# A fourth place for w1's low parts, later transposes of gathered rows, later loads of expert 0's weights, and constant products in TensorE's planned gaps

## The chip, the cores and the metric

The kernel runs on one core of one Trainium2 chip. The metric is the device time of one execution in microseconds (us); lower is better. The engines are called as the profile calls them: PE is TensorE (PEld its weight loads), DVE is VectorE, ACT is ScalarE, POOL is GpSimd and SP is SyncE, whose queue here issues nearly all DMAs.

## The reference

Three stages follow each other: an attention with random features, a dense two-layer block on all 2304 tokens, and a layer of 8 experts with 288 tokens each. Inputs are float32, two dense weight matrices arrive as float64.

```python
# attention: q, k, v are 4 x 8 x 576 x 64, omega 128 x 64
q_p, k_p = phi(q * scale), phi(k * scale)        # exp(x.omega - |x|^2/2 - max) / sqrt(128)
num = q_p @ (k_p^T v);  den = q_p . sum(k_p) + 1e-6
x = (num / den)                                  # 2304 x 512
# dense block: w_in 512 x 2048, w_out 2048 x 512
h = x @ w_in;  x = (h - tanh(h)) @ w_out
# experts: w_gate 512 x 8, w1 8 x 512 x 1024, w2 8 x 1024 x 512
logits = x @ w_gate                              # tokens go to experts in the order of all logits,
                                                 # each expert takes 2304 / 8 = 288 tokens
out[mask_e] = maximum(x[mask_e] @ w1[e], 0) @ w2[e]
```

## The kernel before

Every matrix product is made from three products of high and low parts (high x high, high x low, low x high). So every weight is split: the high part is a rounded copy (ACT), the low part a subtraction (DVE or POOL).

The program is not written in the order in which it runs. Each piece of work is an `op` with an engine (or several to choose from), a planned duration, a priority (`plan.at` plus `lag`), the buffers that it reads and writes and other ops that it follows. `Plan.run` is a list scheduler: it takes the op that can start first by its own model of the engines and issues it. This fixes the order of instructions on each engine; at run time an engine takes them in that order and waits where something is late. Buffers are rings of places (`Ring`), and an op that needs a new buffer waits in the plan until a place is free. `late` adds time to the planned end of an op, and so moves what depends on it back in the plan.

In order of time:

- From 0 to about 125 us: the attention (`unit_ops`), its units mixed with the conversion of the float64 weights (`weight_ops`: DVE reads the bits, ACT makes the high part, DVE or POOL the low part). The key units add into accumulators of the ring `kvr`, of which the first 260 of 512 columns are used.
- To about 533 us: the dense block in 6 blocks of 384 tokens (`mlp_ops`), 16 chunks (f) each: `chunk_ops` makes the hidden values, `m2_ops` (L651) multiplies them with w_out. Blocks 4 and 5 run their first product together, from about 450 us. The products of block 4 with w_out come later, so its low hidden parts go to DRAM, one store for each chunk (`g4l<-gL`, L826). In the same stretch `low_ops` makes the low parts of the first two of four row groups of w1 of all experts, 16 pieces: load of 512 KB (`dw`, L581), two copies on ACT into `dh`, two subtractions on DVE or POOL in place, store to `w1l` (L588). The ring `dw` has 3 places, `dh` 2.
- At about 534 us: a branch (`tc.If`, L1530) that goes to a general version of the dense block when inputs are out of a range; with this input it is passed by. SP's instruction at its end waits for the semaphores of all eight of its DMA queues, that is until everything that SP issued has landed; the other engines go on when SP has.
- To about 622 us: `but_last_ops` and `last_ops`, block 4's and block 5's products with w_out (low parts `oL` loaded from DRAM through 3 places), mixed with the routing of the first expert (`route_ops`: a search whose steps go PE L1096, DVE, PE L1121, DVE) and the second's. When the first expert's tokens are known, POOL gathers their rows (`r_xg`, `xg_rest`, L1351), and PE transposes them (L1369).
- To the end: 8 experts (`expert_ops`), while the next ones are searched for, gathered (L1351, transposes L1364) and their weights loaded (`load_ops`, L1309 to L1330). Expert 0's loads are tied to the loads of `oL` (`oloads`): load number i of its weights follows oL load 2i + 2, the low part follows 2i + 3.

Of the kernel before, what the change touches and what calls it, by code (L numbers as in the profile page):

```python
# [65 lines left out]
class Plan:  # L66
# [6 lines left out]
    def __init__(self):  # L73
        self.ops, self.n, self.at = [], 0, 0.0
        self.free = dict.fromkeys(("PE", "ACT", "DVE", "POOL", "SP", "-"), 0.0)
        self.dma = 0.0
        self.rings = []

    def ring(self, shape, dtype, name, slots):
# [49 lines left out]
    def run(self):  # L129
# [5 lines left out]
        while count:  # L135
# [19 lines left out]
            for b in o.new:  # L155
                if b.slot is not None:
                    continue
                s = self._place(b, (), o.new)
                b.slot, s[4] = s, b
                b.t = s[0].tile(b.ring.shape, b.ring.dtype, tag=s[1], name=s[1], bufs=1)  # L160
            o.fn(e)
            ready.remove(o)
# [24 lines left out]
def tile_kernel(ctx, tc, q, k, v, omega, w_in, w_out, w_gate, w_gate_t, w1, w2, out, dbg=None):  # L187
# [5 lines left out]
    P = 128  # L193
# [110 lines left out]
    def low(e, out, in_, high):  # L304
        (nc.gpsimd if e == POOL else nc.vector).tensor_tensor(out, in_, high.bitcast(F32), op=OP.subtract)  # L305
# [16 lines left out]
    pair = lambda z: z.t.rearrange("p n two -> p (n two)")  # L322
    wbuf, stored_low, first_lo = {}, {}, {}
    bwn, bxn, bhm = Buf(None), Buf(None), Buf(None)

    def weight_ops(kind, f, rings, masked=None):
# [14 lines left out]
        if masked:  # L341
# [3 lines left out]
            plan.op(DVE, 0.6, lambda e: V.copy_predicated(w.t, mk.t.bitcast(I32), masked[1]), r=[w, mk], w=[w])  # L345
        plan.op(ACT, 0.6, lambda e: copy(e, dst.t, w.t), r=[w], w=[dst], lag=6.6)
        plan.op({POOL: 1.4, DVE: 0.7}, 0, lambda e: low(e, lw.t, w.t, dst.t), r=[w, dst], w=[lw], lag=7.3)
# [225 lines left out]
    def low_ops(start, step):  # L573

        n = w1.shape[2]
        d_rings[:] = plan.ring([P, n], F32, "dw", []), plan.ring([P, n // 2], F32R, "dh", [])
        for k in range(E * NPRE):
            e_, r = k // NPRE, slice(k % NPRE * P, (k % NPRE + 1) * P)
            raw = Buf(d_rings[0])
            plan.at = start + step * k  # L580
            plan.op(SP, 0.47, lambda e, raw=raw, e_=e_, r=r: nc.sync.dma_start(raw.t, w1[e_, r, :]), w=[raw], nbytes=P * n * 4,  # L581
                    early=False)
            for i, h in enumerate((slice(0, n // 2), slice(n // 2, n))):
                hi = Buf(d_rings[1])
                plan.op(ACT, 0.6, lambda e, raw=raw, hi=hi, h=h: copy(e, hi.t, raw.t[:, h]), r=[raw], w=[hi], lag=4.0 + 0.6 * i)
                plan.op({POOL: 1.45, DVE: 0.65}, 0, lambda e, raw=raw, hi=hi, h=h: low(
                    e, raw.t.bitcast(F32R)[:, h], raw.t[:, h], hi.t), r=[raw, hi], w=[raw], lag=4.7 + 0.6 * i)
            plan.op(SP, 0.47, lambda e, raw=raw, e_=e_, r=r: nc.sync.dma_start(w1l[e_, r, :], raw.t), r=[raw],  # L588
                    nbytes=P * n * 4, lag=6.8)
# [75 lines left out]

    def gate_ops(j, xms):
        mT, lp, lT, lgb = Buf(mTr), Buf(bank), Buf(sr), Buf(None)
# [20 lines left out]

        plan.op(PE, 0.9, gate, r=[mT, bwg], w=[lp], lag=4.0)
        plan.op({ACT: 0.48, DVE: 0.55}, 0, lambda e: copy(e, lT.t, lp.t[:, :BLK]), r=[lp], w=[lT], lag=5.0)  # L690
# [67 lines left out]
    def mlp_ops(start, step, general=False):  # L758
# [4 lines left out]
        for j in range(NBLK - 1):  # L763
# [34 lines left out]
            plan.at = start[j] + step[j] * NF + LAG2  # L798
            gate_ops(j, xms)

# [498 lines left out]
    def load_ops(p, ei):  # L1299
# [4 lines left out]
        for i in range(2 * NC):  # L1304
# [10 lines left out]
            plan.at = PHASE * p + AT_EW * i + AT_LOAD  # L1315
            turn = [] if p else [oloads[min(2 * i + 2, NF - 1)]]
            plan.op(SP, 0.47, load, w=[raw], after=[o] + turn, nbytes=P * FX * 4)
            plan.at = PHASE * p + AT_EW * i + (AT_SPLIT if p else 0.0)
            plan.op(ACT, 0.98, lambda e, H=H, raw=raw: copy(e, H.t, raw.t), r=[raw], w=[H])
            if i < NPRE:  # L1320
# [3 lines left out]
                plan.at = PHASE * p + AT_EW * i + (AT_SPLIT - 6.0 if p else AT_LOAD)  # L1324
                turn = [] if p else [oloads[2 * i + 3]]
                plan.op(SP, 0.47, load_low, w=[L], after=[o] + turn, nbytes=P * FX * 4)
# [16 lines left out]
    def expert_ops(p):  # L1343
# [4 lines left out]
        for g in range(NG):  # L1348
            t = tmp([GS, DM], F32, "xg", NG - 1) if g < NG - 1 else first["xg"]
            ix = idxs[p][g][1] if p else first["top"][g]  # L1350
            plan.op(POOL, 1.03, lambda e, g=g, t=t, ix=ix: nc.gpsimd.indirect_dma_start(  # L1351
                out=t.t[:GN[g]], out_offset=None, in_=ms if p else ms[:(NTT - TPB) * P + 1, :],
                in_offset=bass.IndirectOffsetOnAxis(ap=ix.t[:GN[g]].bitcast(U32), axis=0)),
                r=[ix], w=[t], after=stored if p else stored4, late=5.0)
            xg.append(t)
# [99 lines left out]

    plan.op(PE, 6.0, warm, w=[idle])
    plan.at = -20.0
    omega_ops()
# [39 lines left out]
    def switch(e):  # L1498
        s_px.close()
        pacc = Lasting(pool(s_acc, "pacc", "right", space=PSUM))  # L1500
        accr.add(pacc, [f"acc{t}" for t in range(TPB)], t=max(o.end for o in early_ops))

    def switch2(e):
        s_att.close()
# [8 lines left out]

    low_ops(starts[-2], (NF * steps[-1] + 4.0) / (E * NPRE))
    plan.at = T_MLP
    plan.op("-", 0.0, switch, after=early_ops)
    mlp_ops(starts, steps)
    att_ops += x_reads
    plan.op("-", 0.0, switch2, after=att_ops)
# [149 lines left out]
```

## Time and profile before

| | |
|---|---|
| time, median of 3 runs | 891.68 us (891.31 to 892.25) |
| the profiled execution's own time | 886.79 us |
| its span, first to last instruction | 884.9 us |
| PE busy | 846.3 us (96%) |
| DVE busy | 654.1 us (74%) |
| ACT busy | 470.2 us (53%) |
| POOL busy | 252.9 us (29%) |

Times below are counted from the span's start. Busy PE is not PE at its peak: the clock that was granted to it has two levels, 1.2 and 2.4 GHz, which the profile shows as 0.5 and 1.0. An engine's wait counts for the end only where nothing later takes it up.

### The profile page before, as it was taken

How to read it: one execution, taken by the hardware profiler on the slowest of the kernel's cores; microseconds unless marked ns; L12 is line 12 of the kernel's file. 1: busy time of each engine (PE TensorE's matmuls, PEld its weight loads, DVE VectorE, ACT ScalarE, POOL GpSimd, SP SyncE). 2: the span in 40 equal slices, each digit the busy share in tenths (PEclk: the TensorE clock that was granted, in tenths of full speed). 3: DMA queues.
4: the chain of work that ended last, by engine and by line, in shares of the span. 5: the costliest groups of instructions: out<-in, count | busy, mean ns of one | idle time of the engine just before them, and what ended most of it. 6: DMA issues, size and time to landing. Idle time of an engine off the chain costs nothing. (4 is left out here: it accounts for less than half of the span.)

```text
span 884.9 us, 17420 instructions
## 1 busy us (share of the span) xinstructions
PE 846.3 (96%) x6116; PEld 756.0 (85%) x6116; DVE 654.1 (74%) x1925; ACT 470.2 (53%) x1021; POOL 252.9 (29%) x276
## 2 busy tenths in 40 slices
PE   8979899999999999999999997989999999999995
PEld 6878788888988888889988985766999988999995
DVE  5898999886588889887887884444887877886520
ACT  4876564744456554755477870012565465455621
POOL 1122344222343345334521251010132322321211
PEclk8999999999999999999999997999999999999998
DMA  8988778887456666633478865567879778877600
GB/s 255 341 259 276 265 240 277 301 264 225 114 184 206 200 191 198 231 100 119 131 265 275 283 229 181 185 230 225 242 233 273 241 207 271 286 207 280 220 27 27
DMA packets 103790, 193.95 MB, mean 219 GB/s; under 512 B 28305, under 2 KB 42257, under 8 KB 103698
## 3 DMA queue, kind: packets, MB, share of 16 engines
q1 hardware_dynamic: 98034, 173.92, 59.7%
q0 software_dynamic: 5664, 18.88, 8.6%
q8 instruction: 49, 0.80, 0.4%
q14 instruction: 43, 0.35, 0.1%
HBM read 149.64 MB, written 33.69 MB: 207 GB/s over the span
## 5 line engine op out<-in xcount | busy, mean ns | idle before, releaser
L604 PE MATMUL bk<-xH,wi 128*128 128x384 f32 x332 | 118.3, 356 | 1.4 <-DVE xt L503 1.1
L605 PE MATMUL bk<-xL,wi 128*128 128x384 f32 x332 | 111.9, 337 | 0.5 <-DVE xL L305 0.5
L606 PE MATMUL bk<-xH,iL 128*128 128x384 f32 x332 | 112.0, 337 | 0.0
L651 PE MATMUL acc<-wo,gL 128*128 128x512 f32 x282 | 111.8, 397 | 0.0
L721 DVE SCALAR_TENSOR_TENSOR lw<-wf,raw 128x512 f32<-128x512 f32 x128 | 107.3, 838 | 5.4 <-POOL wf L718 4.0
L651 PE MATMUL acc<-wo,gH 128*128 128x512 f32 x240 | 99.9, 418 | 0.0
L305 POOL TENSOR_TENSOR gL<-s,gH 128x384 fp32r<-128x384 f32 x49 | 58.1, 1186 | 138.4 <-ACT gH L300 138.4
L441 ACT ACTIVATE phi<-bk,nm 128x128 f32<-128x128 f32 x272 | 77.2, 380 | 36.5 <-DVE nm L444 36.2
L651 PE MATMUL acc<-oL,gH 128*128 128x512 f32 x240 | 95.6, 398 | 0.3 <-DVE oL L305 0.3
L718 POOL TENSOR_TENSOR wf<-oL,wo 128x512 f32<-128x512 f32 x48 | 66.5, 1387 | 66.2 <-DMA oL<-low_wo 55.9
L300 ACT ACTIVATE gH<-s 128x384 fp32r<-128x384 f32 x80 | 42.0, 525 | 62.0 <-DVE s L631 37.1
L604 PEld LDWEIGHTS bk<-xH,wi 128*128 128x128 f32 x332 | 62.9, 189 | 9.0 <-issue 2.0
L629 DVE SCALAR_TENSOR_TENSOR s<-s,bk 128x384 f32<-128x384 f32 x83 | 45.4, 548 | 32.1 <-ACT s L628 31.9
L605 PEld LDWEIGHTS bk<-xL,wi 128*128 128x128 f32 x332 | 62.8, 189 | 3.2 <-DVE xL L305 0.7
L651 PEld LDWEIGHTS acc<-wo,gL 128*128 128x128 f32 x282 | 53.3, 189 | 12.2
L608 ACT ACTIVATE u<-bk 128x384 f32<-128x384 f32 x80 | 39.2, 490 | 44.0 <-PE bk L606 42.7
L606 PEld LDWEIGHTS bk<-xH,iL 128*128 128x128 f32 x332 | 62.6, 189 | 0.0
L631 DVE SCALAR_TENSOR_TENSOR s<-s,u 128x384 f32<-128x384 f32 x80 | 54.6, 682 | 1.1
L444 DVE TENSOR_REDUCE nm<-bk 128x4 f32<-128x512 f32 (+1 forms) x75 | 46.3, 632 | 12.2 <-PE bk L430 11.1
L651 PEld LDWEIGHTS acc<-wo,gH 128*128 128x128 f32 x240 | 45.6, 190 | 7.0 <-issue 0.3
L651 PEld LDWEIGHTS acc<-oL,gH 128*128 128x128 f32 x240 | 45.6, 190 | 6.3 <-DVE oL L305 0.6
L628 ACT ACTIVATE s<-u,qbias 128x384 f32<-128x384 f32 x80 | 49.3, 617 | 2.0
(409 smaller groups left out, 2336.9 us busy)
## 6 DMA issues: line engine op xcount, KB each, us to landing
r_wraw<-in_moe_w_dram SPq DMA_DIRECT2D x50, 512.0 KB, 5.7
iL<-low_wi SPq DMA_DIRECT2D x80, 256.0 KB, 3.3
oL<-low_wo SPq DMA_DIRECT2D x78, 256.0 KB, 2.8
raw<-in_moe_w_in_dram SPq DMA_DIRECT2D x32, 512.0 KB, 5.3
raw<-in_moe_w_out_dram SPq DMA_DIRECT2D x32, 512.0 KB, 4.1
dw<-in_moe_w_dram SPq DMA_DIRECT2D x16, 512.0 KB, 5.3
w1l<-dw SPq DMA_DIRECT2D x16, 512.0 KB, 3.7
s_wraw<-in_moe_w_dram SPq DMA_DIRECT2D x14, 512.0 KB, 6.8
```

The lines of the kernel that those rows point to most:

```text
L305: (nc.gpsimd if e == POOL else nc.vector).tensor_tensor(out, in_, high.bitcast(F32), op=OP.subtract)
L441: nc.scalar.activation(ph.t[:, i0 + i, :], pj.t[:, i * M:(i + 1) * M], AF.Exp, bias=nmx.t[:, i0 + i:i0 + i + 1])
L444: plan.op(DVE, 0.1 + 0.125 * n, lambda e, pj=pj, i0=i0, n=n: V.tensor_reduce(nmx.t[:, i0:i0 + n], pj.t[:, :n * M].rearrange("p (i m) -> p ...
L604: nc.tensor.matmul(ph(), piece(iH, c), xH.t[:, c, :], start=(c == 0), stop=False)
L605: nc.tensor.matmul(ph(), piece(iH, c), xL.t[:, c, :], start=False, stop=False)
L606: nc.tensor.matmul(ph(), piece(iL, c), xH.t[:, c, :], start=False, stop=(c == NC - 1))
L628: plan.op(ACT, 0.52, lambda e: nc.scalar.activation(s.t, ut(), AF.Square, bias=qbias), r=[u], w=[s], lag=2.8)
L629: plan.op(DVE, 0.52, lambda e: V.scalar_tensor_tensor(s.t, s.t, QD, ph(), op0=OP.add, op1=OP.mult), r=[p, s], w=[s], lag=3.4)
L631: plan.op(DVE, 0.65, lambda e: V.scalar_tensor_tensor(s.t, s.t, QC, ut(), op0=OP.mult, op1=OP.mult), r=[u, s], w=[s], lag=4.0)
L651: nc.tensor.matmul(acc[t].t, (gL if k == 2 else gH).t[:, c], (oL if k == 1 else oH).t, start=(f == 0 and k == 0), stop=(f == end and k == ...
L718: plan.op(POOL, 1.45, lambda e: nc.gpsimd.tensor_tensor(w.t, lo.t.bitcast(F32), wo[:, f, :].bitcast(F32), op=OP.add), r=[lo, wbuf["wo", f] ...
L721: x_reads.append(plan.op(DVE, 0.9, lambda e, i=i: nc.vector.scalar_tensor_tensor(scratch.t.bitcast(F32), w.t, 1.0, half(rows[i // 2], i % ...
```

## The change

1. `low_ops` is planned to be done 12 us earlier (its step is computed with -8.0 in place of +4.0), and once block 3's logits are made, the tile `mT` that they were made from becomes a fourth place of the ring `dw`. The two ACT copies of a piece are now planned ahead of its two subtractions, which no longer count as dependent on each other.
2. The gather's planned end is 8.0 us after its issue for expert 0 (5.0 before) and 6.5 us for the others, so the transposes stand later in PE's order.
3. Expert 0's weight loads follow oL loads 2i + 6 and 2i + 7 in place of 2i + 2 and 2i + 3.
4. Until the last weight is converted, where the plan leaves PE idle for over 0.9 us, up to 18 products of constants (128 columns each, bf16) are issued there. They add into columns 384 to 511 of a key accumulator, which nobody reads. In this program there are 42 of them in five places (8, 6, 10, 7 and 11).

```diff
@@ Plan.run
+            if e == "PE" and self.fill and t - self.free[e] > 0.9:
+                self.fill(min(0.4 * (t - self.free[e]), 1.0))
             o.fn(e)
@@ low_ops
-            for i, h in enumerate((slice(0, n // 2), slice(n // 2, n))):
-                hi = Buf(d_rings[1])
+            halves = [(h, Buf(d_rings[1])) for h in (slice(0, n // 2), slice(n // 2, n))]
+            for i, (h, hi) in enumerate(halves):
                 plan.op(ACT, 0.6, lambda e, raw=raw, hi=hi, h=h: copy(e, hi.t, raw.t[:, h]), r=[raw], w=[hi], lag=4.0 + 0.6 * i)
+            for i, (h, hi) in enumerate(halves):
                 plan.op({POOL: 1.45, DVE: 0.65}, 0, lambda e, raw=raw, hi=hi, h=h: low(
-                    e, raw.t.bitcast(F32R)[:, h], raw.t[:, h], hi.t), r=[raw, hi], w=[raw], lag=4.7 + 0.6 * i)
+                    e, raw.t.bitcast(F32R)[:, h], raw.t[:, h], hi.t), r=[hi], rp=[raw], wp=[raw], lag=4.7 + 0.6 * i)
@@ before gate_ops
+    class Whole:
+        def __init__(self, z):
+            self.z = z
+        def tile(self, shape, dtype, tag, **kw):
+            return self.z.rearrange("p c n -> p (c n)")[:, :shape[1]]
@@ gate_ops
-        plan.op(PE, 0.9, gate, r=[mT, bwg], w=[lp], lag=4.0)
+        o = plan.op(PE, 0.9, gate, r=[mT, bwg], w=[lp], lag=4.0)
+        if j == NBLK - 3 and not general:
+            plan.op("-", 0.0, lambda e: d_rings[0].add(Whole(mT.t), ["x"], t=o.end), after=[o])
@@ load_ops
-            turn = [] if p else [oloads[min(2 * i + 2, NF - 1)]]
+            turn = [] if p else [oloads[min(2 * i + 6, NF - 1)]]
...
-                turn = [] if p else [oloads[2 * i + 3]]
+                turn = [] if p else [oloads[2 * i + 7]]
@@ expert_ops, the gather
-                r=[ix], w=[t], after=stored if p else stored4, late=5.0)
+                r=[ix], w=[t], after=stored if p else stored4, late=6.5 if p else 8.0)
@@ tile_kernel
+    def spare(us):
+        accs = [s[4] for s in kvr.slots if s[4] is not None]
+        if accs:
+            fresh = not any(o.done for o in accs[0].writers)
+            for i in range(int(us / 0.055)):
+                nc.tensor.matmul(accs[0].t[:, P * 3:], onev.to_broadcast([P, P]), onev.to_broadcast([P, P]),
+                                 start=fresh and not i, stop=False, skip_group_check=True)
+    plan.fill = spare
...
+    def switch1(e):
+        plan.fill = None
...
-    low_ops(starts[-2], (NF * steps[-1] + 4.0) / (E * NPRE))
+    low_ops(starts[-2], (NF * steps[-1] - 8.0) / (E * NPRE))
...
+    plan.op("-", 0.0, switch1, after=[high_op["wo", NF - 1]])
```

The first place is SP's queue just ahead of the branch, before the change; `w1l<-dw` stores a low part of w1, `dw<-` loads the next piece, `g4l` are block 4's hidden low parts.

```order
L588 DMA w1l<-dw_6360 128x1024
L826 DMA g4l_92<-gL_6488 128x384
L826 DMA g4l_93<-gL_6506 128x384
L588 DMA w1l<-dw_6400 128x1024
L581 DMA dw_6533<-in_moe_w_dram 128x1024
L588 DMA w1l<-dw_6457 128x1024
L826 DMA g4l_94<-gL_6541 128x384
L588 DMA w1l<-dw_6533 128x1024
L1529 TENSOR_LOAD over
```

The same place of the changed kernel (its lines 584, 592 and 841 are 581, 588 and 826 of before).

```order
L584 DMA dw_6438<-in_moe_w_dram 128x1024
L841 DMA g4l_90<-gL_6448 128x384
L841 DMA g4l_91<-gL_6462 128x384
L592 DMA w1l<-mT_5732 128x1024
L841 DMA g4l_92<-gL_6508 128x384
L592 DMA w1l<-dw_6378 128x1024
L841 DMA g4l_93<-gL_6542 128x384
L592 DMA w1l<-dw_6438 128x1024
L841 DMA g4l_94<-gL_6557 128x384
L1558 TENSOR_LOAD over
```

The last load of w1 stood behind the store `g4l_93` and its own store was SP's last instruction; now the load stands ahead of `g4l_90`, four stores of `g4l` earlier, and the last instruction is the store `g4l_94`.

The second place is PE's order at the transposes of expert 0's gathered rows, before the change; the rows of L1096 and L1121 are the first step of the second expert's search, `acc` takes block 5's products with w_out.

```order
L1096 MATMUL rp_12294<-r_cmp_12279,pairs_11722 128x62
L1121 LDWEIGHTS d_987
L1121 MATMUL rp_12310<-id_985,d_987 128x8
L1369 MATMUL bd_12323<-ident,r_xg_12235 128x128
L1369 MATMUL bd_12323<-ident,r_xg_12251 128x128
L1369 MATMUL bd_12323<-ident,xg_rest 128x128
...
L651 MATMUL acc_1408<-wo,gH_5_5950 128x512
```

The changed kernel at this place (its line 1111 is 1096 of before, 655 is 651 and 1384 is 1369).

```order
L1111 MATMUL rp_12326<-r_cmp_12306,pairs_11761 128x62
L655 MATMUL acc_1450<-wo,gH_5_5996 128x512
L655 MATMUL acc_1450<-oL_12302,gH_5_5996 128x512
...
L655 MATMUL acc_1455<-oL_12332,gH_7_6111 128x512
L1384 MATMUL bd_12365<-ident,r_xg_12272 128x128
L1384 MATMUL bd_12365<-ident,r_xg_12286 128x128
L1384 MATMUL bd_12365<-ident,xg_rest 128x128
```

23 products of block 5 now stand between the search's first five counts and the transposes; the other four counts and L1121 of that step come after them.

The third place is SP's queue in `last_ops`, before the change: `low_wo` are the loads of `oL`, `r_wraw` and `r_ewL` the first of expert 0's weights (512 KB each).

```order
L566 DMA oL_12188<-low_wo_140 128x512
L1309 ISA
L1309 DMA r_wraw_12214<-in_moe_w_dram 128x1024
L1322 ISA
L1322 DMA r_ewL_12240<-w1l 128x1024
L1309 ISA
L1309 DMA r_wraw_12254<-in_moe_w_dram 128x1024
L566 DMA oL_12269<-low_wo_141 128x512
```

The changed kernel from the same load on (its line 569 is 566 of before, 1324 is 1309 and 1337 is 1322).

```order
L569 DMA oL_12227<-low_wo_140 128x512
L569 DMA oL_12302<-low_wo_141 128x512
L569 DMA oL_12319<-low_wo_142 128x512
L569 DMA oL_12332<-low_wo_143 128x512
L1324 ISA
L1324 DMA r_wraw_12343<-in_moe_w_dram 128x1024
L569 DMA oL_12347<-low_wo_144 128x512
L1337 ISA
L1337 DMA r_ewL_12353<-w1l 128x1024
L569 DMA oL_12362<-low_wo_145 128x512
L1324 ISA
L1324 DMA r_wraw_12382<-in_moe_w_dram 128x1024
```

Three loads of expert 0's weights, 1.5 MB, stood together ahead of the oL load of chunk 5; now one at a time stands between the oL loads from chunk 8 on.

## Rows read from the trace of the kernel before

**Rows 1.** The page's part 1: busy us (share of the span) and instructions of each engine.

```profile
PE   846.3 (96%) x6116; PEld 756.0 (85%) x6116; DVE 654.1 (74%) x1925; ACT 470.2 (53%) x1021; POOL 252.9 (29%) x276
```

**Rows 2.** PE's waits: line and releaser, us in total, times, longest.

```profile
PE acc L651 <- SPq L1530: 3.9, 1, 3.9
PE bk L430 <- DVE s L629: 3.1, 1, 3.1
...
PE be L1364 <- DMA r_xg<-ms,r_ig: 1.3, 2, 1.1
PE be L1364 <- DMA xg_rest<-ms,r_ig: 0.7, 2, 0.6
```

**Rows 3.** Stretches: us, busy PE PEld DVE ACT POOL, PEclk, DMA share, GB/s.

```profile
12.80:19.63 6.83, 6.83 (x49) 6.71 (x49) 4.55 (x10) 3.07 (x10) 1.64 (x3) 0.50 1.12 314
...
450.00:525.00 75.00, 73.84 (x430) 67.75 (x429) 60.85 (x97) 59.98 (x121) 22.16 (x19) 1.00 0.78 268
...
539.09:545.30 6.21, 6.21 (x22) 4.72 (x23) 0.74 (x4) 0.00 (x0) 2.53 (x8) 0.50 0.65 206
...
589.72:593.13 3.41, 3.41 (x10) 2.73 (x9) 0.00 (x0) 0.52 (x1) 0.00 (x0) 0.51 0.26 105
```

**Rows 4.** SP's issues in order of time, 528 to 540 us: start, duration, line.

```profile
528.62 0.43 SPq L581 DMA_DIRECT2D dw<-in_moe_w_dram  x1
...
532.02 0.43 SPq L826 DMA_DIRECT2D g4l<-gL  x1
535.05 0.34 SPq L588 DMA_DIRECT2D w1l<-dw  x1
539.93 0.34 SPq L855 DMA_DIRECT2D gL<-g4l  x1
```

**Rows 5.** The page's DMA issues: count, KB each, median us from issue to landing.

```profile
oL<-low_wo SPq DMA_DIRECT2D x78, 256.0 KB, 2.8
...
w1l<-dw SPq DMA_DIRECT2D x16, 512.0 KB, 3.7
```

**Rows 6.** PE in order of time at the branch: start, duration, [idle before <-releaser].

```profile
532.64 0.72 PE L746 MATMUL bk<-ident,lt 16*128 16x16 f32 x6 [0.22 <-ACT lt L300]
534.70 0.47 PE L651 MATMUL acc<-wo,wi 128*128 128x512 f32 x1 [1.33 <-PEq L1530]
539.09 0.79 PE L651 MATMUL acc<-xm,wi 128*128 128x512 f32 x1 [3.93 <-SPq L1530]
```

**Rows 7.** PE in order of time at expert 0's gathered rows, 583 to 590 us.

```profile
583.12 0.39 PE L651 MATMUL acc<-wo,gH 128*128 128x512 f32 x1
...
584.26 0.39 PE L651 MATMUL acc<-wo,gL 128*128 128x512 f32 x1
584.49 0.44 PE L1096 MATMUL rp<-r_cmp,pairs 128*128 128x62 bf16 x9
585.48 0.18 PE L1121 MATMUL rp<-id,d 128*128 128x8 bf16 x1 [0.56 <-DVE r_cond L1117]
587.55 0.33 PE L1369 MATMUL bd<-ident,r_xg 128*128 128x128 f32 x1 [1.89 <-DMA r_xg<-ms,r_ix]
588.72 0.33 PE L1369 MATMUL bd<-ident,r_xg 128*128 128x128 f32 x1 [0.84 <-DMA r_xg<-ms,r_ix]
```

**Rows 8.** DVE in order of time: block 4's and 5's low hidden parts.

```profile
524.94 1.37 DVE L305 TENSOR_TENSOR gL<-s,gH 128x384 fp32r<-128x384 f32 x1
...
531.46 0.55 DVE L305 TENSOR_TENSOR gL<-s,gH 128x384 fp32r<-128x384 f32 x1
```

**Rows 9.** Expert 0's last low part of w1: POOL in order of time.

```profile
603.98 0.99 POOL L1330 DMA_DIRECT2D wi<-r_wraw  x1 [20.51 <-ACT wi L1329]
```

**Rows 10.** DMA issues of 570 to 640 us: count, KB, median us to landing.

```profile
r_wraw<-in_moe_w_dram SPq DMA_DIRECT2D x12, 512.0 KB, 5.5
...
s_ewL<-r_wraw POOLq DMA_DIRECT2D x1, 512.0 KB, 9.3
```

**Rows 11.** PE's first product with expert 0's weights, in order of time.

```profile
622.49 0.38 PE L1402 MATMUL bd<-r_xgH,wi 128*128 128x288 f32 x1
```

More of the change, by code (lines that the diff above doesn't have):

```diff
@@ L77, in __init__ @@
         self.rings = []
+        self.fill = None
     def ring(self, shape, dtype, name, slots):
@@ L322, in tile_kernel @@
     pair = lambda z: z.t.rearrange("p n two -> p (n two)")
-    wbuf, stored_low, first_lo = {}, {}, {}
+    wbuf, stored_low, first_lo, high_op = {}, {}, {}, {}
     bwn, bxn, bhm = Buf(None), Buf(None), Buf(None)
@@ L345, in weight_ops @@
             plan.op(DVE, 0.6, lambda e: V.copy_predicated(w.t, mk.t.bitcast(I32), masked[1]), r=[w, mk], w=[w])
-        plan.op(ACT, 0.6, lambda e: copy(e, dst.t, w.t), r=[w], w=[dst], lag=6.6)
+        high_op[kind, f] = plan.op(ACT, 0.6, lambda e: copy(e, dst.t, w.t), r=[w], w=[dst], lag=6.6)
         plan.op({POOL: 1.4, DVE: 0.7}, 0, lambda e: low(e, lw.t, w.t, dst.t), r=[w, dst], w=[lw], lag=7.3)
@@ L664, in out_ops, with gate_ops @@
                            nbytes=P * DM * 4)
-    def gate_ops(j, xms):
+    class Whole:
[3 more added lines that the diff above has]
+            return self.z.rearrange("p c n -> p (c n)")[:, :shape[1]]
+    def gate_ops(j, xms, general):
         mT, lp, lT, lgb = Buf(mTr), Buf(bank), Buf(sr), Buf(None)
@@ L798, in mlp_ops @@
             plan.at = start[j] + step[j] * NF + LAG2
-            gate_ops(j, xms)
+            gate_ops(j, xms, general)
         j, lacc4, lprev4 = NBLK - 2, Buf(bank), None
```

## The prediction

> **What bounds the kernel now.** I read the page's busy times first: PE is busy for 846.3 of 884.9 us and DVE, the next, for 654.1 [rows 1]. So the end is set by PE's work plus the time in which PE stands still or runs at the lower clock, and I listed its waits. The longest is 3.9 us in one piece, for SP [rows 2]. In order of time it stands at the branch: PE's last work before it begins at 532.64, its first product behind it at 534.70, and the second only at 539.09, after 3.93 us for SP [rows 6]. SP's queue tells why. Its last DMA ahead of the branch is a store of a w1 low part, issued at 535.05, and its next DMA comes at 539.93 [rows 4]. Such a store lands 3.7 us after issue in the median [rows 5], which is 538.75, and PE goes on 0.34 us later. SP waits at the branch's end for everything that it issued, so the last store's landing holds all engines.
>
> The second place is expert 0's gathered rows: after the search's step waits 0.56 us for DVE, the transposes wait 1.89 and 0.84 us for the gather [rows 7].
>
> I then asked for the granted clock behind both. From 539.09 to 545.30, 6.21 us, PE is busy at 0.50, and from 589.72 to 593.13, 3.41 us, at 0.51 [rows 3]. A product at half the clock takes twice as long, so these stretches cost 3.1 and 1.7 us more than they had to. There is such a stretch at the start too, 12.80 to 19.63 [rows 3]. The rest of PE's waits behind the branch are small: 1.3 and 0.7 us at later experts' gathers [rows 2].
>
> **The change part by part.**
>
> *Branch, the wait.* The last w1 load was issued at 528.62 and its store at 535.05, the last one [rows 4]. In the new order that load stands ahead of four stores of block 4's low hidden parts (`g4l`), which come once per chunk, and SP's last DMA is the store `g4l` of chunk 13. That one was issued at 532.02 [rows 4]. Its landing has no row. It moves 192 KB, so I bound it by 2.8 us (256 KB, oL) and 3.7 us (512 KB, w1l) [rows 5]: it lands at 534.82 to 535.72, and PE may go on 0.34 later, at 535.16 to 536.06 in place of 539.09. The gain is 3.9 to 3.0 us; I take 3.4. If a w1 store is still late it is 0. It can't pass 4.16: PE's own branch lets its first product start at 534.70, and that takes 0.23 (below).
>
> *Branch, the clock.* PE's pause behind its last small products shrinks from 5.7 us (533.36 to 539.09) to some 2.3, which is nearest to what PE stood still at the gather (3.3 us), and that was followed by 3.41 us at the lower clock [rows 3, 7]. Bounds: the clock stays (gain 3.1), falls for as long as now (0), falls as behind the gather (3.1 - 1.7 = 1.4). I take 1.4, the nearest row.
>
> *Gather of expert 0.* 23 products now stand between the search's first counts and the transposes. Five products lie 1.14 us apart from 583.12 to 584.26 [rows 7], so one takes 0.228 us and 23 take 5.2. The counts begin at 584.49 and nine take 0.44, so PE reaches the transposes at about 590.0, and the last gathered row that it had to wait for was there at 588.72 [rows 7]. That leaves 1.3 us. Gained are 1.89 + 0.84, the 0.56 for DVE (the step's second half now stands behind products) and 1.7 of clock: 5.0 us. Three loads of 1.5 MB also leave SP's queue ahead of the gather, which can only help it. Against it: from chunk 8 on a 512 KB load stands ahead of an oL load. Through 3 places, oL is requested only when a chunk's products are done, about 9 x 0.228 = 2 us each. The price of a delayed oL load lies between 0 and what a 512 KB load takes longer, 5.5 - 2.8 = 2.7 us [rows 5, 10], for a first one that is not yet ahead; I take 0.5. Net 4.5.
>
> *Expert 0's weights later.* POOL started the last low part of w1 at 603.98, such a DMA takes 9.3 us, and PE's first product with these weights is at 622.49 [rows 9 to 11]: 9.2 us to spare. PE arrives some 5 us earlier and that load stands at most two oL loads, about 4 us, later. Cost 0, but the cover is thin: beyond that each us late is a us of PE.
>
> *Later gathers.* 1.5 us more is planned. Of the 2.0 us [rows 2] all may go, or as much may return elsewhere, since transposes that stand later make their copies later. I take 1.0.
>
> *Low parts earlier.* The same 32 subtractions run in a shorter time. By the order six low hidden parts go from POOL to DVE, at 0.55 to 1.37 us each [rows 8]: 3.3 to 8.2 us, and one w1 subtraction comes back to POOL. From 450 to 525 us DVE is busy 60.85 of 75 us and PE 73.84 [rows 3]: 14.2 us of DVE's idle time cover it. Cost 0 to PE.
>
> *Constant products.* 42 of 128 columns. The nearest row is the counts: nine of 62 columns in 0.44 us [rows 7], 0.05 each, so at most 0.1 for twice the columns, 4.2 us in all if none falls into a real gap. On the other side they could keep the clock up at the start, 6.83 us at 0.50 [rows 3], worth 3.4. I take 0: the attention's PE waits for DVE anyway, 3.1 us in one piece behind four of the five places in the order [rows 2], and no row shows that so few products hold the clock. The Trainium skill, "TensorE: Matmul & The Clock Gate", section "Back-to-back issue gap", gives about 81 ns for one product of 128 columns with its weight load; that would be 42 x 0.081 = 3.4 us, and the sum below would be 6.9 if all of it lay on the path. No such product is in this trace; the row's bound is a little above it.
>
> **Sum**: 3.4 + 1.4 + 4.5 + 1.0 = 10.3 us. Against the profiled execution, 886.8 (span 884.9 and 1.9 around it), that gives 876.5. The runs' median is 891.7, 4.9 above; the same saving gives **881.4**.
>
> **The rivals.**
>
> *The branch stays held.* A w1 store or a `g4l` store behind it is still in flight late, because ACT and DVE are dense up to the end. For it: the pieces were paced by three places and by engines that serve the hidden values too. Against: the load stands four chunk stores earlier. Then 4.8 us are missing: 886.2.
>
> *The gather's wait turns into waits for oL.* PE no longer pauses, so the oL loads have no pause to catch up, and each now has a 512 KB load beside it. For it: only three places. Against: PE never waits for oL now. Price up to the 4.5 us of that term: 885.9.
>
> *The constant products lie on the path.* PE takes products in program order, so they delay a ready one behind them. For it: the planned gap ahead of the second group is not there in the stretch at 0.50, where PE is busy for the whole 6.83 us [rows 3]. Against: DVE's waits behind it. Price up to 4.2: 885.6. The same page of the Trainium skill, section "Step-by-step: what each phase is for", states the order: only weight loads are pulled ahead, products stay in program order; no row here shows one that overtakes another.
>
> *The other side, slower.* SP's queue is in order. In block 4 and 5 a store of a low part that waits for its subtraction stands ahead of loads of `iL`, which PE needs for every chunk. With pieces planned every 3.6 us, (64.8 - 8) / 16, in place of 4.3, (64.8 + 4) / 16, SP falls behind, and PE waits in each of 16 chunks. It decides from 10.3 / 16 = 0.64 us per chunk; at 0.9 it is 14.4 - 10.3 = 4 us slower, 895.8. Against: PE lost only 1.2 of 75 us there [rows 3].
>
> *It does nothing*: the dense block gives back what the branch gains and the gather's gap reappears as another: 891.
>
> **How the numbers follow.** Chances: forecast 0.56 (own range 877.5 to 884.5: gains from 7 to 14, the latter with 3.9, 3.1, 5.0 and 2.0), branch held 0.12, oL 0.10, constant products 0.08, nothing 0.07, slower 0.07. The range goes down to 876.5, the four upper bounds and a little of the start's clock, and up to 888.5, two rivals at once being 890.7 and single ones 886: outside are nothing, slower and some of the pairs. No change and a change under 0.2% (1.8 us) can't be told apart here. Faster are the forecast, the three single losses and little else, 0.85; same 0.08; slower 0.07.
>
> **What would show it.** Right: SP's wait on PE below 1.2 us with the last SP store before the branch a `g4l`; less than 6.2 us at 0.50 behind it; transposes L1369 without a wait for DMA, and no stretch at 0.5 behind them; PE still above 73 of 75 us busy in block 4 and 5. Wrong: a w1 store as last to land, PE waits for `oL` or `iL` loads, waits at expert 0's first products, or PE later than before at the attention's end.

## The result and the profile after

The changed kernel takes 877.59 us in the median of 4 runs (876.01 to 880.86), the kernel before 891.49 beside it; the ratio is 0.985 with a 95% interval of 0.9817 to 0.9883. The forecast was 881.4 (own range 877.5 to 884.5, so the measured median lies 0.1 us inside its lower end). The profiled execution took 876.29 us, its span is 874.5 against 884.9: 10.4 us of span where the sum said 10.3. That the two agree so closely is luck, as the parts below show.

The changed kernel's page, part 1 (compare [rows 1]): PE is still the engine that sets the end.

```profile
PE   845.2 (97%) x6158; PEld 754.0 (86%) x6158; DVE 652.2 (75%) x1933; ACT 468.4 (54%) x1018; POOL 247.0 (28%) x271
```

Its PE waits (line and releaser, us in total, times, longest). Of [rows 2] the wait for SP at the branch is gone and so are those for gathered rows; DVE's 3.1 us in the conversion stayed.

```profile
PE bk L433 <- DVE s L633: 3.1, 1, 3.1
...
PE acc L655 <- PEq L1559: 0.8, 1, 0.8
...
PE rp L1136 <- DVE r_cond L1132: 0.5, 3, 0.2
```

**The branch.** SP's issues of the changed kernel from 530 us on (compare [rows 4]): the last w1 store leaves at 530.17, in place of 535.05, and the last instruction ahead of the branch is a `g4l` store.

```profile
530.17 0.34 SPq L592 DMA_DIRECT2D w1l<-dw  x1
530.87 0.32 SPq L841 DMA_DIRECT2D g4l<-gL  x1
537.84 0.34 SPq L870 DMA_DIRECT2D gL<-g4l  x1
```

PE in order of time there (compare [rows 6]): no wait for SP, the second product starts at 537.56 and not at 539.09. But PE comes to the branch later: its last small products start at 535.39, before at 532.64. SP is through the branch ahead of them now (its eight semaphore waits, first the changed kernel's, then those of before):

```profile
L1559 SPq EVENT_SEMAPHORE  x8: 17/17/17, 534.2 to 534.8; - x8
L1530 SPq EVENT_SEMAPHORE  x8: 17/17/17, 539.0 to 539.6; - x8
```

The rows of PE:

```profile
533.20 0.34 PE L750 MATMUL kv<-gL,vgs 128*8 128x384 f32 x1 [0.55 <-POOL gL L308]
533.38 0.34 PE L748 MATMUL bk<-wi,vgs 128*16 128x384 f32 x1
534.47 0.34 PE L750 MATMUL bk<-gLk,vgs 128*8 128x384 f32 x1 [0.75 <-POOLq L1559]
...
535.39 0.77 PE L761 MATMUL bk<-ident,lt 16*128 16x16 f32 x6 [0.15 <-ACT lt L303]
537.00 0.76 PE L655 MATMUL acc<-wo,wi 128*128 128x512 f32 x1 [0.84 <-PEq L1559]
537.56 0.63 PE L655 MATMUL acc<-xm,wi 128*128 128x512 f32 x1
```

**The gather.** At expert 0's rows PE pauses nowhere (compare [rows 7]): the transposes start at 586.70; before, the first came at 587.55 and the second at 588.72.

```profile
581.19 0.32 PE L1111 MATMUL rp<-r_cmp,pairs 128*128 128x62 bf16 x5
...
586.47 0.40 PE L655 MATMUL acc<-oL,gH 128*128 128x512 f32 x1
586.70 0.38 PE L1384 MATMUL bd<-ident,r_xg 128*128 128x128 f32 x2
```

Stretches of the changed kernel (us, busy PE PEld DVE ACT POOL, PEclk, DMA share, GB/s; compare [rows 3]). PE works at half the clock for 3.40 us behind the branch in place of 6.21, and the stretches behind the gather and from 12.80 us are gone (near 62 us it has one of 6.8 us, where before has one of 3.4 near 64). In block 4 and 5 PE is as busy as before.

```profile
450.00:525.00 75.00, 74.11 (x426) 67.12 (x424) 59.29 (x100) 57.72 (x118) 14.77 (x13) 1.00 0.82 284
12.80:19.63 6.83, 6.83 (x88) 6.54 (x86) 6.79 (x13) 4.50 (x15) 1.61 (x4) 1.00 1.12 322
...
537.00:540.40 3.40, 3.40 (x8) 2.71 (x9) 2.07 (x7) 0.00 (x0) 2.53 (x8) 0.52 0.42 114
...
586.00:593.00 7.00, 7.00 (x41) 5.53 (x39) 0.43 (x3) 2.12 (x2) 0.00 (x0) 1.00 0.86 288
```

Each sign that the prediction had named for a right forecast is there. Which part of the change brings which gain, a single trace can't tell; the experiments had to.

### The profile page after: what moved, and what is told of

The parts are those of the page before. It is cut to its first block, busy times and chain, and to the rows that moved or that the text cites. A ratio compares the mean times of both kernels' runs of the same rounds, so it can differ in the third digit from the quotient of the medians.

```text
span 874.5 us, 17508 instructions
## 1 busy us (share of the span) xinstructions
PE 845.2 (97%) x6158; PEld 754.0 (86%) x6158; DVE 652.2 (75%) x1933; ACT 468.4 (54%) x1018; POOL 247.0 (28%) x271
## 5 line engine op out<-in xcount | busy, mean ns | idle before, releaser
L635 DVE SCALAR_TENSOR_TENSOR s<-s,u 128x384 f32<-128x384 f32 x80 | 51.8, 648 | 1.3
```

The costliest lines, as they stand in the source:

```text
L635: plan.op(DVE, 0.65, lambda e: V.scalar_tensor_tensor(s.t, s.t, QC, ut(), op0=OP.mult, op1=OP.mult), r=[u, s], w=[s], lag=4.0)
```

## The experiments

Twelve runs were made in three groups (e, f, and g with c0, which is before again), each group beside runs of the kernel before on its own chip: medians 890.95, 890.62 and 888.66. The e and f groups ran on one chip, the third on another. So kernels of different groups are compared by ratio, which is taken over all runs and need not agree with that of the medians. "Routing" is the time from PE's first search count (L1096 of before, L1111 of the changed kernel; 544.0 and 541.4) to its first product with expert 0's weights (L1402 and L1417; 622.5 and 612.4), "experts" from there to the span's end. Both are of the one profiled execution, which is not always a typical one: those of before, f1, f4 and f7 are the fastest of their kernels, those of e1 and c0 the slowest.

| kernel | median us | ratio, 95% interval | routing | experts |
|---|---|---|---|---|
| before | 891.49 | 1 | 78.5 | 262.4 |
| changed | 877.59 | 0.985 [0.9817, 0.9883] | 71.1 | 262.1 |
| e1_no_fill | 877.93 | 0.9858 [0.9819, 0.9896] | 71.3 | 263.9 |
| e2_no_part1 | 881.37 | 0.9892 [0.9856, 0.9929] | 71.0 | 262.9 |
| e3_late_5 | 878.30 | 0.986 [0.9825, 0.9895] | 71.1 | 263.2 |
| e4_turn_as_before | 887.54 | 0.9976 [0.9947, 1.0004] | 75.8 | 265.2 |
| f1_part1_only | 887.28 | 0.9976 [0.9954, 0.9997] | 76.9 | 266.6 |
| f7_turn_only | 880.25 | 0.9877 [0.985, 0.9903] | 71.0 | 263.5 |
| f3_late_both_only | 892.76 | 1.0018 [0.9993, 1.0042] | 80.3 | 269.5 |
| f4_step_only | 895.32 | 1.0032 [1.001, 1.0055] | 76.9 | 267.8 |
| g1_loads_twice | 879.53 | 0.9887 [0.9865, 0.9909] | 75.9 | 258.7 |
| g2_part1_turn | 873.32 | 0.9828 [0.9809, 0.9847] | 71.1 | 258.7 |
| g4_fill_more | 877.48 | 0.9871 [0.9848, 0.9894] | 71.3 | 260.4 |
| c0_before_again | 889.10 | 1.0004 [0.9983, 1.0025] | 79.9 | 268.5 |

### Each part taken out of the change

The changed kernel without the constant products:

```diff
-    plan.fill = spare
```

> The changed kernel without its 42 constant products; every other instruction and the order are those of the changed kernel. My theory (they are worth nothing for the end): at 20 us PE is 2 us later again and the stretch at half the clock from 12.8 us is back, but the float64 conversion on DVE takes that up before 150 us, so the time is that of the changed kernel, 877.6 within 1.2 us. Rival A (the constant products hold the clock and that reaches the end): 2 us of the start and perhaps a second stretch near 60 us, 879.6 to 881. Rival B (they lie on PE's path): 42 at the 0.08 us that the trace shows (8 in 0.64 us) are 3.4 us, so 874.2.

877.93 us: no worth for the end is shown, as my theory had it; a difference below some 0.4% would not show. The profiled execution, the slowest of its six (885.21), had 17.1 us at half the clock in the conversion, so its total says nothing of the products.

The changed kernel with part 1 undone (three places, +4.0, copy and subtraction in turn):

```diff
-    low_ops(starts[-2], (NF * steps[-1] - 8.0) / (E * NPRE))
+    low_ops(starts[-2], (NF * steps[-1] + 4.0) / (E * NPRE))
...
-        if j == NBLK - 3 and not general:
-            plan.op("-", 0.0, lambda e: d_rings[0].add(Whole(mT.t), ["x"], t=o.end), after=[o])
```

> The changed kernel with the making of w1's low parts as before: three places, the older pace, and each subtraction planned behind its own copy. My theory: SP's last instruction ahead of the branch is a store of w1's low part again, PE waits for SP for over 3 us, and the time is 3.2 (PE's lead behind the branch in the two profiles) to 4.8 us (the forecast's two branch terms) over the changed kernel's: 880.8 to 882.4. Rival (the wait only moved, since PE reached the branch's first product 2.3 us later in the changed kernel): under 1.5 us, 879.1 at most.

881.37 us, 3.8 slower, inside the expected range. Its PE waits show the branch held again:

```profile
PE acc L654 <- SPq L1556: 3.8, 1, 3.8
```

The changed kernel with the gather's planned end as before:

```diff
-                r=[ix], w=[t], after=stored if p else stored4, late=6.5 if p else 8.0)
+                r=[ix], w=[t], after=stored if p else stored4, late=5.0)
```

> The changed kernel with the gather's planned end at 5.0 us again for all experts (so the transposes stand early in PE's order); the weight loads stay where the change put them. My theory: PE waits for the gather again, 2.5 to 3.3 us, followed by a stretch of 3.4 us at half the clock, and later gathers cost 1 us: 4.5 to 6.7 us, 882.1 to 884.3. Rival (it was the loads taken out from ahead of the gather in SP's queue that ended the wait, not the later place): under 1.5 us, 879.1 at most, with a gather wait under 1 us.

878.30 us, 0.7 more: my theory fell, the rival held. No PE wait for expert 0's gather is in its list. In its row order 11 products still stand between the counts and the transposes, where before had none there: with the loads moved the planner itself puts the transposes later.

The changed kernel with expert 0's weight loads where they were:

```diff
-            turn = [] if p else [oloads[min(2 * i + 6, NF - 1)]]
+            turn = [] if p else [oloads[min(2 * i + 2, NF - 1)]]
...
-                turn = [] if p else [oloads[2 * i + 7]]
+                turn = [] if p else [oloads[2 * i + 3]]
```

> The changed kernel with expert 0's weight loads tied to the oL loads 2i + 2 and 2i + 3 as before. My theory: these loads only add traffic ahead of the gather and the transposes now stand far behind it; the time stays at 877.6 within 1.2 us. Rival A (three loads of 512 KB together ahead of an oL load make PE wait for oL or delay the gather now that PE no longer pauses): 2 to 4 us slower, 879.6 to 881.6, with PE waits named oL or the gather. Rival B (loads late in the changed kernel cost something at expert 0): faster by 0.5 to 1.5 us.

887.54 us, 10 slower, far past my theory (no change) and past rival A's price. So the part that I had priced at nothing carries most of the gain. PE's waits in this profile are small pieces:

```profile
PE rp L1136 <- DVE r_cond L1132: 3.5, 9, 0.9
...
PE rp L1111 <- DVE r_cmp L1105: 2.7, 5, 0.8
...
PE acc L655 <- DMA oL<-low_wo: 0.8, 1, 0.8
```

### Each part alone on the kernel before

Part 1 alone (the reverse of e2's edit):

> The kernel before with the changed making of w1's low parts alone (fourth place, earlier pace, copies ahead of subtractions). Theory: it is worth the same alone as inside the change (its undoing cost 3.8 us): SP's last instruction ahead of the branch is a store of g4l, no PE wait for SP there, 891.0 - 3.8 = 887.2, between 886.2 and 887.8. Rival (with the loads of expert 0's weights still ahead of the gather, being earlier at the branch is given back at the gather): 889.5 to 891.

887.28 us; 3.3 by the medians, 2.1 (0.3 to 4.1) by the ratio. The wait for SP is gone as expected, but expert 0's gather still stops PE, 1.8 us in two waits from 530 to 625 us:

```profile
PE bd L1381 <- DMA r_xg<-ms,r_ix: 0.9, 1, 0.9
PE bd L1381 <- DMA xg_rest<-ms,r_ix: 0.9, 1, 0.9
```

The later loads alone:

```diff
-            turn = [] if p else [oloads[min(2 * i + 2, NF - 1)]]
+            turn = [] if p else [oloads[min(2 * i + 6, NF - 1)]]
...
-                turn = [] if p else [oloads[2 * i + 3]]
+                turn = [] if p else [oloads[2 * i + 7]]
```

> The kernel before with the later loads of expert 0's weights alone (tied to oL loads 2i + 6 and 2i + 7). Theory, changed by the first runs: it is these loads, 512 KB each on the same DMA engines as the gather, that delay the gather and the oL loads; alone the edit takes away the gather's wait and its stretch at half the clock (4.4 us) and up to 5 us more by 720 us: 881.5 to 886.5. Rival (it needs the later transposes too): the gather's wait stays over 1.5 us and the time is 889 or more.

880.25 us: 10.4 faster by the medians, 11.0 by the ratio, a little past the theory's range. PE at the gather, in order of time, with `late` still 5.0: no wait, and the counts are followed by 10 products and then the transposes.

```profile
581.09 0.32 PE L1096 MATMUL rp<-r_cmp,pairs 128*128 128x62 bf16 x5
583.65 0.38 PE L1369 MATMUL bd<-ident,r_xg 128*128 128x128 f32 x2
```

The later transposes alone:

```diff
-                r=[ix], w=[t], after=stored if p else stored4, late=5.0)
+                r=[ix], w=[t], after=stored if p else stored4, late=6.5 if p else 8.0)
```

> The kernel before with the later transposes alone (gather's planned end 8.0 us for expert 0, 6.5 us for the others). My forecast's step: no gather wait at expert 0, 4.5 us of gain and 1.0 at later gathers, 885.5 to 886.5. Rival from the first runs (undoing it cost 0.7 us only): the gather's wait does go, but PE waits for oL and for the search instead, since the loads of 512 KB are still in their way: 889.5 to 891.

892.76 us, no gain. The gather's wait did go, but two others came in its place. From 536 to 625 us PE now waits for `oL`:

```profile
PE acc L651 <- DMA oL<-low_wo: 2.8, 2, 1.8
```

and from 622 us on, where the later experts' gathers have no wait any more, for the search that stands mixed with them:

```profile
PE rp L1121 <- DVE r_cond L1117: 3.8, 8, 1.4
PE rp L1096 <- DVE r_cmp L1090: 3.6, 5, 1.2
```

The earlier pace alone, without a fourth place:

```diff
-    low_ops(starts[-2], (NF * steps[-1] + 4.0) / (E * NPRE))
+    low_ops(starts[-2], (NF * steps[-1] - 8.0) / (E * NPRE))
```

> The kernel before with the earlier pace of w1's low parts alone (-8.0 in place of +4.0 in its step; three places). Theory: with three places the pieces are held by the ring, SP's last ten rows ahead of the branch read as before, and the time is 891 within 1 us with the PE wait for SP near 3.9 us. Rival (the pace is what matters): over 2.5 us faster, at most 888.5.

895.32 us. PE waits for SP 3.9 us as in before, so pace without a place doesn't free the branch. That it is slower than before by 0.1 to 0.55% neither theory had. The profile shows no cause: it is of the fastest execution (888.62), and PE's row order from expert 0's first product on is that of before, row for row. This stays open.

### Transfers or order

The later loads alone, but with the first three loads also issued at their old place. PE, DVE, ACT and POOL have the rows of f7_turn_only, in the same order:

```diff
+            if not p and i < 2:
+                plan.op(SP, 0.0, load, w=[raw], after=[o, oloads[2 * i + 2]])
...
+                if not p and i < 1:
+                    plan.op(SP, 0.0, load_low, w=[L], after=[o, oloads[2 * i + 3]])
```

> The kernel before with the later loads of expert 0's weights, but the first three of them (512 KB each) are also issued at their old place, into the same buffers, and then once more at the new place. PE, DVE, ACT and POOL have row for row the order of the run with the later loads alone (880.25 us); SP has three loads more. Theory (the transfers themselves, ahead of the gather and of oL loads, are what costs): the gather lands later, PE waits there or for oL, and at least 3 us of the 10.4 go: 883.5 to 888. Rival (the edit helps by the other order that the planner makes with it): 880.25 within 1.2 us.

879.53 us, ratio 0.9887 against 0.9877: by the time, the theory fell and the rival's bounds were met. The ratios differ by 0.9 us, with about 3 us of uncertainty to either side. The place that the theory named did move. Routing is 4.9 us longer with the same rows (75.9 against 71.0): PE waits for `oL`, and half the clock follows over the transposes. PE in order of time, then a stretch:

```profile
586.78 0.50 PE L651 MATMUL acc<-oL,gH 128*128 128x512 f32 x1 [2.80 <-DMA oL<-low_wo]
...
589.58 0.63 PE L1373 MATMUL bd<-ident,r_xg 128*128 128x128 f32 x2
```

```profile
588.50:591.60 3.10, 3.10 (x13) 2.70 (x13) 0.00 (x0) 1.06 (x1) 0.00 (x0) 0.50 0.49 165
```

So the three transfers do stop PE in the routing, but in this profile the experts' stage was 4.8 us shorter than in f7_turn_only's (258.7 against 263.5). That is not the stage giving the wait back. PE's rows from expert 0's first product on stand in one order in e3_late_5, f7_turn_only, g1_loads_twice and g2_part1_turn (below). The stage took 263.2 and 263.5 us in the first two, on one chip, and 258.7 in both of the last two, on the other chip.

On its own chip g1 is best set beside g2. Their profiles differ by 2.3 us ahead of the first count, 4.8 in the routing and nothing in the experts' stage, their medians by 6.2 us. g2 also has part 1, worth 2.1 to 3.8 us in e2 and f1, which leaves an estimated 2.4 to 4.1 us to the transfers. f7_turn_only itself didn't run on that chip, so what the three transfers cost at the end stays open, between the 0.9 us of the ratios and these 4.1.

### The other sizes

The two parts that had shown a gain, on the kernel before (part 1 and the later loads):

> The kernel before with two parts of the change alone: w1's low parts (fourth place, pace, order of copies) and the later loads of expert 0's weights; transposes planned as before, no constant products. Theory: the single gains add up, 890.7 - 3.3 - 10.4 = 877.0, between 876 and 878.5, as fast as the whole change. Rival (the later transposes or the constant products do add something inside the whole): 879.5 to 881.

873.32 us, faster than expected, in part because the expectation counted from 890.7 and this group's before is at 888.66. By ratio the gain is 15.3 us, where the two single gains add up to 13.1. Its ratio, 0.9828, lies below that of the changed kernel, 0.985, with overlapping intervals. In its own group it beats g4_fill_more, which has the later transposes and 110 constant products as well, by 4.2 us; so there the two add nothing and may cost something, and which of them is not shown. PE's row order is e3_late_5's but for the 42 products; whether these cost the difference (0.9828 against 0.986) is not settled, since e1 shows no such cost.

The changed kernel with 110 constant products:

```diff
-            if e == "PE" and self.fill and t - self.free[e] > 0.9:
-                self.fill(min(0.4 * (t - self.free[e]), 1.0))
+            if e == "PE" and self.fill and t - self.free[e] > 0.5:
+                self.fill(min(0.8 * (t - self.free[e]), 3.0))
```

> The changed kernel with 110 constant products in place of 42: wherever the plan leaves PE idle for over 0.5 us, for 0.8 of it and up to 3 us. Theory (they are worth nothing in the median, only the clock's stretches move): 877.6 within 1.5 us. Rival A (they hold the clock): the stretch at half the clock near 62 to 69 us goes, up to 2 us at the end of the conversion, 875.5. Rival B (they lie on the path): 68 more at 0.07 to 0.08 us each (8 in 0.64, 6 in 0.52) are 5 us, 882.5.

877.48 us. By ratio, since the groups' chips differ, none, 42 and 110 of them give 0.9858, 0.985 and 0.9871, with overlapping intervals: no difference is shown. The first group in the changed kernel's trace, and what follows it:

```profile
9.04 0.64 PE L1478 MATMUL kv<-onev 128*128 128x128 bf16 x8
9.52 1.06 PE L464 MATMUL kv<-v,phi 128*128 128x65 f32 x8
```

The next product starts 0.48 us after the first of the eight, so one takes 0.06 us of PE, where my bound from the counts was 0.1. The 0.08 us of the expectations divide the row's length, 0.64 us, which also holds the time until the last product is through. The Trainium skill, "TensorE: Matmul & The Clock Gate", section "Back-to-back issue gap", had 81 ns; the trace gives less.

The kernel before, profiled once more:

> The kernel before once more, with a profile of its own. The profile on which the forecast rests gave 886.8 us while the timed runs' median is 890.7. Theory: the runs differ in the experts' stage (first product with expert 0's weights to the end), 262.4 us there and 265 to 268 us in the profiles of the other kernels with early loads; in this profile it is over 264. Rival: they differ ahead of it, in stretches at half the clock in the conversion: the experts' stage is 262 to 263.5 and its start is later than 624.

The theory held: this execution took 894.12 us, routing and experts 79.9 and 268.5 us. PE's waits from 584 us on, and two stretches in the experts' stage:

```profile
PE be L1364 <- DMA xg_rest<-ms,r_ig: 4.9, 2, 3.0
PE bd L1369 <- DMA r_xg<-ms,r_ix: 3.2, 2, 2.4
```

```profile
714.40:717.80 3.40, 3.40 (x23) 3.34 (x24) 1.36 (x6) 2.46 (x6) 0.00 (x0) 0.51 0.52 100
816.80:820.20 3.40, 3.26 (x15) 3.26 (x16) 1.76 (x4) 1.65 (x4) 0.00 (x0) 0.51 0.10 37
```

The same rows in the same order lose at least 4.9 us at later gathers, against 0.7 + 1.3 in [rows 2]. But this execution is the slowest of its eight (887.84 to 894.12), as the one on which the forecast rests (886.79) lies below all four timed runs beside it (890.33 to 892.25). The two show how far executions of before can differ in this stage, not what a typical one loses there.

## Why the prediction was right, and where not

**The total** holds, 877.59 for 881.4, but partly by luck: terms stood in for each other, and the gain in the medians is 13.9 us where the sum had 10.3. In the two profiles 2.6 us come from ahead of the first search count (forecast 4.8), 7.4 from the routing (4.5) and 0.3 from the experts (1.0).

**Branch, the wait (3.4) and the clock (1.4).** The mechanism is shown: e2 brings the wait back, f1 alone takes it away. Only "holds all engines" says too much: in before, PE's first product behind the branch runs at 534.70 [rows 6] and DVE's first row there at 535.51; PE's second product and POOL wait for SP. The landing that "has no row" has one, inside the bounds taken:

```profile
g4l<-gL SPq DMA_DIRECT2D x14, 192.0 KB, 2.9
```

The size was too large: the lead behind the branch is 3.2 us, not 4.8 (the first search step's second half, L1136, at 543.11 against 546.32). The wait gave 1.5 (537.56 for 539.09), because PE itself comes 2.75 us later (535.39 for 532.64); the half clock gave the 1.4 forecast (3.40 us for 6.21, half of the difference). The step that failed is "low parts earlier: cost 0". I set the work against DVE's idle time of all 75 us from 450 to 525; it fell due in the last 15. From 520 to 534.7 DVE is busy 13.92 us, before 12.72, and the tail's small products wait for `gL`, the longest two for parts that POOL made (0.55 and 0.75 us, the second shown as POOLq). First before, then the changed kernel:

```profile
520.00:534.70 14.70, 12.97 (x69) 9.62 (x66) 12.72 (x20) 9.37 (x19) 8.06 (x6) 1.00 0.65 242
520.00:534.70 14.70, 12.46 (x66) 9.35 (x64) 13.92 (x20) 10.54 (x21) 9.21 (x7) 1.00 0.46 175
```

The 14 profiles settle that part 1 does this. I count from one product that all of them have, the 313th of the 332 `bk<-xH,wi` (511.39 us in before, 511.10 in the changed kernel). The last small products start 21.3 us behind it in all seven without part 1, f4 with the earlier pace alone among them, and 24.3 us behind it in all seven with it; PE's idle time in between is 0.4 and 2.4 us. So the step priced at 0 cost 3.0 us of what the freed branch gave.

**Gather of expert 0 (4.5).** The gain was seen in the right place and credited to the wrong part. The later transposes alone gain nothing (f3), and without them the gain stays (e3). What works is part 3, of which I wrote that it "can only help" the gather and costs 0 later. Alone it gains 11.0 us by the ratio, and undoing it costs 10. The seven kernels with the loads in the later place only have a routing of 71.0 to 71.3 us, the six profiles with the early ones 75.8 to 80.3, and g1 shows that the three transfers alone, with the same rows, make it 4.9 us longer. So of f7's gain in the routing, 7.5 us in the two profiles, the transfers explain 4.9; the other order of the rows is left for the rest, which is not shown. The rival "the gather's wait turns into waits for oL" is what f3 shows. It didn't befall the change, which moved the loads too; with the loads put back (e4) a wait of 0.8 us for `oL` and waits for the search return, and the routing is 4.7 us longer.

**Experts.** Outside the forecast. The median of the profiles is 262.9 us with the later loads (changed, e1, e2, e3, f7, g2, g4: 258.7 to 263.9) and 267.2 with the early ones (before twice, f1, f3, f4, e4: 262.4 to 269.5). The planner orders this stage differently when the loads move: of PE's 2225 rows from expert 0's first product on in before, 1421 stand in the same order in f7_turn_only. The three early transfers don't lengthen the stage: g1 with them and g2 without have one order and 258.7 us both. That the order makes it shorter is argued from this, not shown, since the other loads of expert 0 move as well. A longer experts' stage of before would also explain why the medians fell by 13.9 us where the profiles' spans fell by 10.4: c0 shows that an execution of before can lose gathers and clock there that its first profile didn't lose, but c0's is a slow one.

**Later gathers (1.0).** Their waits are gone in the changed kernel, yet its experts' stage is only 0.3 us shorter than before's in the profiles, and alone the edit turns them into waits for the search (f3): no worth is shown.

**Expert 0's weights later (0).** No PE wait for them in any kernel with late loads. **Constant products (0)**: nothing against it at none, 42 and 110, within some 0.4%.

## What to carry to other kernels

When a load is taken from ahead of a latency-bound gather, price both the transfer and the place: here three loads of 512 KB cost 4.9 us of routing in the profiles, and moving the loads gained some 10 us (f7), the new order that came with it included, while moving the waiting instruction alone only handed the wait to other queues (f3). Idle time of an engine covers added work only in the stretch where that work falls due. And a sum made on one profile should be checked against a second profile of the same kernel before its terms are believed to a few us.

## What was not expected of the hardware

With constant products in it (five profiles: changed, e2, e3, e4, g4) the kernel had one single stretch at half the clock ahead of the branch, 6.8 us near 62 us. Without them (nine profiles) there were one to three, of 3.4 to 17.1 us, and two profiles of the same kernel differ: before has 12.80 to 19.63 [rows 3], c0 none there. So in these profiles the few products go with one and the same course of the clock. They aren't needed for it: g1 and g2 have none, and the same single stretch of 6.8 us near 62 us. Where the stretches are short, little is left of them: PE's first products of the dense block's chunks lie within 0.4 us of each other in before and the changed kernel from 123 to 508 us.

The longest, of e1_no_fill, came while PE was busy for 16.41 of 17.10 us, and ahead of it for 1.79 of 2.00:

```profile
32.20:49.30 17.10, 16.41 (x85) 15.34 (x83) 9.70 (x35) 7.55 (x21) 2.54 (x2) 0.50 0.85 268
30.00:32.00 2.00, 1.79 (x13) 1.29 (x12) 1.93 (x5) 2.00 (x9) 0.11 (x1) 1.00 1.07 348
```

There PE was 6.7 us behind the changed kernel at 158 us, and 8.9 us at the end: this long one was not taken up.
